# The first mixture of an attention and expert kernel in six units of unequal width instead of eight of 288 tokens

## The chip, the cores and the metric

The kernel runs on one core of one Trainium2 chip. The metric is the device time of one execution in microseconds; the time before is the median of three runs. The profile is of one execution of its own. PE is the matrix engine, PEld its weight load, DVE the vector engine, ACT the scalar engine, POOL the general engine and SP the engine that issues most DMAs.

## The reference

2304 tokens (4 batches of 576) go through three stages. Attention has 8 heads of 64; heads 0 to 3 see the last 32 positions, heads 4 to 7 every 32nd position. Then a dense mixture with 2048 hidden columns, then eight experts with 1024 hidden columns, one for each token.

```python
scores = np.where(masks[None, :, :, :], scale * np.matmul(q, k.transpose(0, 1, 3, 2)), -1000000000.0)
attn = np.exp(scores - np.max(scores, axis=-1, keepdims=True))
attn = attn / (np.sum(attn, axis=-1, keepdims=True) + 1e-09)
x = np.matmul(attn, v)                      # then heads side by side: 2304 x 512
r = np.maximum(x @ w_in, 0.0)               # first mixture, 512 x 2048
x = (s * (r * r) + b) @ w_out               # 2048 x 512
...
e_idx = np.argmax(x @ w_gate, axis=1)       # second: one of 8 experts a token
ye = np.maximum(x[mask] @ w1[e], 0.0) @ w2[e]
out[mask] = gate_w[mask, None] * eom[mask, e, None] * ye
```

## The kernel before

One Python generator stands for each stream of work, and a planner (`Order`, line 123) takes the operation that can begin first by its own table of costs and due times. It writes the instructions of every engine in that order, so each engine's order is fixed when the program is built, and the engines meet at semaphores.

**Attention** goes in 28 rounds, seven a batch (`rounds_of`, line 94): three strided ones ("S") of four blocks and four local ones ("L") of 3, 2, 2 and 2 blocks of 64 queries. A round (`attn`, line 426) has mask and score matmuls (L455 to L462), a softmax on DVE and ACT, transposes on PE (L511), the value product (L547, L549) and copies into `xsl`, high and low part (L572, L589). Rounds in `EXPB` take the exponentials on ACT, 64 or 96 columns at a time, the others in one piece with two more DVE operations. Rounds 7 and later are held back until a given step of the mixture has begun (`PACE1` to `PACE4`). The store `xsl` holds two batches of 576 columns, by the batch's parity.

**The first mixture** (`moe1`, line 696) works on units of U = 288 tokens, half a batch, eight of them, and for each unit on 16 blocks of 128 hidden columns, so 128 steps. A step is twelve matmuls into `h` (L713: four blocks of the depth by three passes, high by high, high by low, low by high) and, a step later, twelve into four accumulators (L743: again three passes). Between the two `chain` (L671) makes g = relu squared from h: ACT relu (L674), ACT square (L679), ACT copy that rounds to the high part (L686), DVE subtraction for the low part (L688). g comes from `NG` = 3 buffers, r from three. The weights come as 64-bit numbers and are cut to 32 bits and split by three to five DVE and ACT operations a tile (`split_w64`, L646 to L634); 32 tiles are needed in steps 0 to 23. Unit 0 does eight steps, then unit 1 all sixteen, then unit 0 the rest.

**After a unit** `finish` (L782) takes the four accumulators out (L803, L805), stores them, and `gates` (L815) splits each quarter to xh high and low (L824 or L826, L829), which takes a g buffer, multiplies it with the gate weights (L843, `wgt` of 128 columns of which 32 are used), and transposes the logits (L859). The planner puts a quarter's gate matmuls no sooner than `GLAT` after the split.

**The second mixture** (`dense`, line 1050) does one predicted expert for all tokens in groups of 384 (L1065 with 384 columns, L1090 and L1109 with 512 or 256); the rest of the tokens go through small extra work at the end.

**Idle PE** is filled by the planner with matmuls on zeros (`warm`, `filler`, L1399): 138 of 288 columns, all ahead of the first step.

Of the kernel before, what the change touches and what calls it, by code (L numbers as in the profile page):

```python
# [6 lines left out]
F32 = mybir.dt.float32  # L7
# [14 lines left out]
QT = 96  # L22
TPU = 3
# [7 lines left out]
PRED_UNIT = 4  # L31
# [11 lines left out]
U = S // 2  # L43
NU = NT // U
NEG = -8589934592.0
NQV = 2
NG = 3
# [22 lines left out]
EXPB = range(0, 14)  # L70
# [3 lines left out]
GLAT = 2.5  # L74
PACE1 = 9.0
PACE2 = 3.1
PACE3 = 28.0
PACE4 = 4.1
# [25 lines left out]
GPB = len(GROUPS) // B  # L104
# [134 lines left out]
def body(ctx, tc, qkv, w12, moe_s, moe_b, wg, e12, out):  # L239
# [8 lines left out]
    at = at_ctx.enter_context(tc.tile_pool(name="at", bufs=2))  # L248
    ps = enter(tc.tile_pool(name="ps", bufs=2, space=PSUM))

    xd = [dram.tile([P, KD, U], F32, name=f"xd{u}") for u in range(NU)]
# [13 lines left out]
    wgt = const.tile([P, KD, P], F32R, name="wgt")  # L265
# [9 lines left out]
    xsl = mx.tile([P, 8, 2, S], F32R, name="xsl", tag="big", bufs=1)  # L275
# [70 lines left out]
    t_g, t_r, t_raw, t_x1, t_x2 = Tok(NG), Tok(3), Tok(3), Tok(1), Tok(2)  # L346

    def prep():
        nc.vector.memset(ones, 1.0)
        nc.vector.memset(wgt.bitcast(F32), 0.0)  # L350
        one = mx.tile([P, P], F32, name="one", tag="r", bufs=3)
# [5 lines left out]
        mf = mx.tile([P, 2 * LK + QB], F32, name="mf", tag="r", bufs=3)  # L357
# [37 lines left out]
    for g, (kind, b, i0, n) in enumerate(GROUPS):  # L395
        us = {2 * b, 2 * b + 1}
        if kind == "L":
            us = {2 * b + i0 * QB // U, 2 * b + ((i0 + n) * QB - 1) // U}
        xuses.append(us)
        for u in us:  # L400
            left[u] += 1
# [18 lines left out]
    def xs(b):  # L420
        return xsl[:, 2 * (b % 2):2 * (b % 2) + 2, :, :]

    def xl(b):
        return xsl[:, 4 + 2 * (b % 2):6 + 2 * (b % 2), :, :]

    def attn(g):
# [13 lines left out]
        step = int(PACE1 + PACE2 * (g - GPB)) if g < 2 * GPB - 2 else int(PACE3 + PACE4 * (g - 2 * GPB + 2))  # L440
        step = -1 if g < GPB else step
# [22 lines left out]
        if g + 1 < len(GROUPS):  # L464
            o.spawn(attn(g + 1), prio=P_ATT if g + 1 < GPB else P_ATT2, pe=P_ATT)
# [32 lines left out]
        nt = n if strided else 2 * n  # L498
        yield op(("PE", nt * 0.09 + 0.02), waits=[singles if strided else pairs, t_w if early else t_ph])
        toks = o.got[0:1] if strided else o.got[0:2]  # L500
        ph, ph_tok = buf("ph")
        nj = n // 2 if strided else n
        ph = ph[:, 0:2 * nj * P].rearrange("p (h j k) -> p h j k", h=2, k=P)
        if strided:
            pt = banks_of(toks)[0].rearrange("p (h j k) -> p h j k", h=2, k=P)
        else:
            pt = two_banks(toks)[:, :, 0:nj * P].rearrange("p h (j k) -> p h j k", k=P)
        for j in range(nj):
            for h in range(2):
                src = pr[:, h, 2 * j:2 * j + 2, :].rearrange("p i k -> p (i k)") if strided else pr[:, h, j, :]  # L510
                nc.tensor.transpose(out=pt[0:nk, h, j, :], in_=src, identity=ident)  # L511
        o.free(pr_tok)
        yield op(("ACT", 2 * nj * P / 1200 + 0.19), ("DVE", 2 * nj * P / 960 + 0.12, P_EVAC), on=toks)
        if o.eng == "ACT":
            nc.scalar.activation(out=ph[0:nk], in_=pt[0:nk], func=AF.Copy)
        else:
            nc.vector.tensor_copy(out=ph[0:nk], in_=pt[0:nk])
        for tok in toks:
            o.free(tok)
        if strided:  # L520
            nq = [min(SQ, max(0, (STRIDE - (i0 + i) * CPB) * CLS)) for i in range(n)]
            last = 2 * b + 1
        else:
            nq = [QB] * n
            last = 2 * b + ((i0 + n) * QB - 1) // U
        deps = [ev_l1[last - 4]] if b >= 2 else []
# [32 lines left out]
        if strided:  # L559
            for r in range(2):  # L560
                r0 = (i0 + 2 * r) * CPB
                nr = sum(nq[2 * r:2 * r + 2]) // CLS
                src = ogs[r][:, 0:2 * P].rearrange("p (a x) -> p a x", a=2)[:, :, 0:nr * CLS]
                runs.append((toks[r], 2 * nr * CLS, src.rearrange("p a (r j) -> p a j r", j=CLS),
                             [xs(b)[:, hl].rearrange("q a (j r) -> q a j r", r=STRIDE)[:, :, :, r0:r0 + nr] for hl in range(2)]))
        else:
            src = ogs[0][:, 0:2 * n * QB].rearrange("p (a t) -> p a t", a=2)
            runs.append((toks[0], 2 * n * QB, src, [xl(b)[:, hl, :, i0 * QB:(i0 + n) * QB] for hl in range(2)]))
        for tok, nn, src, dst in runs:
# [20 lines left out]
            o.free(tok)  # L590
# [48 lines left out]
    def split_w64(j):  # L639
# [5 lines left out]
        a = mx.tile([P, 512], I32, name="w64", tag="wraw", bufs=3)  # L645
# [14 lines left out]
    def xt(u, c, hl):  # L660
        b, hf = divmod(u, 2)
        if c < 2:
            return xl(b)[:, hl, c, hf * U:(hf + 1) * U]
        return xs(b)[:, hl, c - 2, hf * U:(hf + 1) * U]

# [5 lines left out]
    def chain(k, u, h, ev, box):  # L671
        yield op(("ACT", 0.42), waits=[t_r])
        r = mx.tile([P, U], F32, name="r", tag="r", bufs=3)
        nc.scalar.activation(out=r, in_=h, func=AF.Relu)  # L674
        yield op(("DVE", 0.45), ("ACT", 0.43, P_SQ))
# [5 lines left out]
        yield op(("ACT", 0.43), waits=[t_g])  # L681
# [813 lines left out]
```

## Time and profile before

| what | us |
|---|---|
| median of three runs (733.22 to 733.96) | 733.46 |
| profiled execution, its own time | 732.7 |
| its span, first to last instruction | 731.0 |
| PE busy | 723.0 |
| DVE busy | 337.1 |
| ACT busy | 303.3 |
| first step of the first mixture starts at | 40.44 |
| second mixture starts at | 509.39 |

The span is read from the first instruction to the last. A group's row has its count, its busy time, the mean of one instruction and the idle time of the engine ahead of it with what ended it. A matmul's mean length is longer than the distance to the next one, since matmuls overlap; the distance is read from starts in the timeline. DMA packets took 26.4% of the 16 engines' span.

### The profile page before, as it was taken

Reading aid. Unit: us, or ns where it says so; the run is one execution under the profiler, and the core shown is the slowest. Engines: PE = TensorE matmul, PEld = TensorE weight load, DVE = VectorE, ACT = ScalarE, POOL = GpSimd, SP = SyncE. Lnnn points to the kernel's source line nnn. Section 1 sums busy time; section 2 is a strip of 40 time slices with the busy share of each in tenths; the row PEclk is TensorE's granted clock in tenths of the full one; section 3 lists DMA queues with packets and bytes.
Section 4 is the critical chain, followed back from the end, with each engine's and each line's share of the span. In section 5 each row is a group of like instructions: output and inputs, shape, how many; then the busy total and the mean of one; then the engine's idle time right before and its main releaser. Section 6 shows DMA issues by size and latency. Waiting matters only on the chain. (4 is left out here: it accounts for less than half of the span.)

```text
span 731.0 us, 14606 instructions
## 1 busy us (share of the span) xinstructions
PE 723.0 (99%) x5969; PEld 686.8 (94%) x5969; DVE 337.1 (46%) x818; ACT 303.3 (41%) x791; POOL 11.1 (2%) x67
## 2 busy tenths in 40 slices
PE   9999999999999999999999999999999999999996
PEld 7899999999999999999999999999999999888995
DVE  6998887444434434433542311751457513522220
ACT  5766655654445345444444444673221212111111
POOL 1000000000000000000000000000000000000001
PEclk9999999999999999999999999999999999999999
DMA  8953550303211122111100200560012297001011
GB/s 328 397 187 141 201 164 12 116 16 108 80 54 49 31 88 76 40 39 47 49 16 1 77 1 2 153 197 1 32 2 87 57 357 257 2 1 44 1 44 46
DMA packets 39113, 65.82 MB, mean 90 GB/s; under 512 B 12862, under 2 KB 21183, under 8 KB 39043
## 3 DMA queue, kind: packets, MB, share of 16 engines
q1 hardware_dynamic: 38882, 64.58, 26.4%
q8 instruction: 48, 0.79, 0.5%
q0 software_dynamic: 160, 0.28, 0.1%
q14 instruction: 23, 0.18, 0.1%
HBM read 54.64 MB, written 10.32 MB: 89 GB/s over the span
## 5 line engine op out<-in xcount | busy, mean ns | idle before, releaser
L713 PE MATMUL h<-xsl,w 128*128 128x288 f32 x1536 | 231.9, 297 | 0.0
L743 PE MATMUL bk<-g,w 128*128 128x288 f32 (+1 forms) x1524 | 230.4, 298 | 0.0
L713 PEld LDWEIGHTS h<-xsl,w 128*128 128x128 f32 x1536 | 211.5, 188 | 1.6
L743 PEld LDWEIGHTS bk<-g,w 128*128 128x128 f32 x1524 | 210.1, 189 | 2.1
L688 DVE TENSOR_TENSOR g<-r,g 128x288 fp32r<-128x288 f32 x128 | 58.6, 457 | 154.9 <-ACT g L686 141.7
L674 ACT ACTIVATE r<-h 128x288 f32<-128x288 f32 x128 | 52.6, 411 | 171.4 <-PE h L713 171.3
L1065 PE MATMUL h<-x,w 128*128 128x384 f32 x576 | 107.6, 336 | 0.0
L1065 PEld LDWEIGHTS h<-x,w 128*128 128x128 f32 x576 | 100.8, 188 | 3.2
L1090 PE MATMUL bk<-w,ht 128*128 128x512 f32 x360 | 90.8, 395 | 0.0
L1018 ACT ACTIVATE ht<-h 128x384 fp32r<-128x384 f32 x48 | 23.6, 491 | 149.7 <-PE h L1065 149.7
L1090 PEld LDWEIGHTS bk<-w,ht 128*128 128x128 f32 x360 | 66.5, 188 | 12.5 <-issue 0.6
L1020 DVE SCALAR_TENSOR_TENSOR ht<-h,ht 128x384 fp32r<-128x384 f32 x48 | 26.8, 558 | 102.1 <-ACT ht L1018 98.4
L686 ACT ACTIVATE g<-r 128x288 fp32r<-128x288 f32 x128 | 56.9, 444 | 14.7 <-PE bk L743 7.7
L679 ACT ACTIVATE r<-r 128x288 f32<-128x288 f32 x126 | 56.0, 444 | 3.9
L471 DVE TENSOR_REDUCE sm<-bk 128x4 f32<-128x384 f32 (+2 forms) x28 | 17.9, 641 | 27.3 <-PE bk L462 27.3
L479 ACT ACTIVATE pr<-bk,sm 128x64 f32<-128x64 f32 (+1 forms) x84 | 26.2, 329 | 0.3
L1399 PE MATMUL warm<-wgt 128*96 128x288 f32 x138 | 23.2, 316 | 1.7 <-DVE wgt L350 1.7
L1399 PEld LDWEIGHTS warm<-wgt 128*96 128x96 f32 x138 | 19.7, 173 | 2.7 <-DVE wgt L350 1.7
L649 DVE SCALAR_TENSOR_TENSOR w<-raw,w 128x512 int32<-128x512 int32 x32 | 21.9, 685 | 0.2
L652 DVE SCALAR_TENSOR_TENSOR w<-raw,w 128x512 int32<-128x512 int32 x32 | 21.9, 685 | 0.1
L549 PEld LDWEIGHTS bk<-ph,qkv 64*64 64x64 f32 (+1 forms) x600 | 17.4, 135 | 3.9 <-issue 2.1
L549 PE MATMUL bk<-ph,qkv 64*64 64x54 f32 (+1 forms) x600 | 20.8, 225 | 0.0
(175 smaller groups left out, 528.1 us busy)
## 6 DMA issues: line engine op xcount, KB each, us to landing
raw<-w SPq DMA_DIRECT2D x32, 512.0 KB, 8.0
qkv<-qkv SPq DMA_DIRECT2D x24, 256.0 KB, 2.9
qkv<-qkv SPq DMA_DIRECT2D x12, 512.0 KB, 4.8
xd<-x SPq DMA_DIRECT2D x8, 576.0 KB, 3.1
X<-xd SPq DMA_DIRECT2D x8, 576.0 KB, 7.3
out<-ob SPq DMA_DIRECT2D x17, 256.0 KB, 3.4
wraw<-e SPq DMA_DIRECT2D x16, 256.0 KB, 3.8
we<-e SPq DMA_DIRECT2D x8, 512.0 KB, 8.3
```

Of the source, the lines that this page charges most:

```text
L479: nc.scalar.activation(out=pr[:, h, i, :], in_=sc[:, h, i, :], func=AF.Exp, scale=0.125, bias=v[2][:, j:j + 1], accum_out=v[1][:, j:j + 1])
L549: nc.tensor.matmul(out=dst, lhsT=lhs, rhs=rhs)
L674: nc.scalar.activation(out=r, in_=h, func=AF.Relu)
L679: nc.scalar.activation(out=r, in_=r, func=AF.Square)
L686: nc.scalar.activation(out=gt[:, 0, 0:U], in_=r, func=AF.Copy)
L688: nc.vector.tensor_sub(out=gt[:, 1, 0:U], in0=r, in1=gt[:, 0, 0:U].bitcast(F32))
L713: nc.tensor.matmul(out=h, lhsT=w_t[2 * fc][:, a, c * P:(c + 1) * P], rhs=xt(u, c, x), start=(c == 0 and n == 0), stop=(c == KD - 1 and n = ...
L743: nc.tensor.matmul(out=acc[pu][c], lhsT=w_t[2 * pf + 1][:, a, c * P:(c + 1) * P], rhs=gt[:, x, 0:cols(pu)], start=(first and n == 0), stop ...
L1020: nc.vector.scalar_tensor_tensor(out=ht[:, 1, :], in0=h, scalar=0.0, in1=ht[:, 0, :].bitcast(F32), op0=ALU.max, op1=ALU.subtract)
L1065: nc.tensor.matmul(out=h, lhsT=w_t["p", 2 * fc][:, a, c * P:(c + 1) * P], rhs=x2[s][:, x, c, :], start=(c == 0 and n == 0), stop=(c == KD ...
L1090: nc.tensor.matmul(out=acc2[q][t][0], lhsT=pbox[0][:, x, t * P:(t + 1) * P], rhs=w_t["p", 2 * pf + 1][:, a, :], start=(pf == 0 and n == 0) ...
L1399: nc.tensor.matmul(out=t[0:3 * P // 4, 0:9 * P // 4], lhsT=wgt[:, 0, P // 4:], rhs=wgt[:, 0:3, P // 4:])
```

## The change

The eight units become six, of 288, 288, 384, 480, 384 and 480 tokens. Units 2 and later no longer end at batch borders, so a round's tokens can fall into two units. `xsl` is one strip of two regions: local heads 1056 columns, strided heads 1344, and `COL` says where each unit stands; units that are no longer read are overwritten, and `segments` gives for each round the pieces, their columns and the units that must be done before. Batches 1 to 3 have three local rounds of three blocks instead of four (25 rounds in all), and late local rounds transpose in two halves of one bank. A table `PACE` gives the step that holds each round back, and `EXPB` ends at round 9. The g, r and weight-raw buffers go from three to two. `GLAT` goes from 2.5 to 0.5. The unit's output tile `x1` gets a pool of its own, whose space the second x2 tile takes over after the last unit. The gate weights shrink to 32 columns, and the filler matmuls have 256 columns. Costs of operations in the planner follow the unit's width. The second mixture is as before.

```diff
-TPU = 3
+USZ = (288, 288, 384, 480, 384, 480)
+UOF = tuple(sum(USZ[:k]) for k in range(len(USZ) + 1))
+UMAX = max(USZ)
...
-NG = 3
+NG = 2
+NR = 2
+NRAW = 2
...
-EXPB = range(0, 14)
+EXPB = range(0,10)
...
-GLAT = 2.5
-PACE1 = 9.0
-PACE2 = 3.1
-PACE3 = 28.0
-PACE4 = 4.1
+GLAT = 0.5
+PACE = dict(zip(range(7, 25), (9, 12, 15, 18, 21, 32, 34, 36, 38, 40, 42, 48, 50, 53, 56, 59, 64, 69)))
...
+    even = [("L", b, i, 3) for i in (0, 3, 6)]
...
-    return early + strided + late if b == 0 else strided + early + late
+    return early + strided + late if b == 0 else strided + even
...
+WIDE = {"S": 1344, "L": 1056}
+COL = {"S": (192, 480, 864, 0, 480, 864), "L": (0, 288, 672, 96, 576, 0)}
...
+def segments(kind, t0, t1):
+
+    out = []
+    while t0 < t1:
+        u = unit_of(t0)
+        n = min(t1, UOF[u + 1]) - t0
+        c = COL[kind][u] + t0 - UOF[u]
+        dead = {v for v in range(u) if COL[kind][v] < c + n and c < COL[kind][v] + USZ[v]}
+        if out and out[-1][1] + out[-1][2] == c:
+            out[-1] = out[-1][0], out[-1][1], out[-1][2] + n, out[-1][3] | dead
+        else:
+            out.append((t0, c, n, dead))
+        t0 += n
+    return out
+
+
...
+    x1p = x1_ctx.enter_context(tc.tile_pool(name="x1p", bufs=1, side="right"))
...
-    wgt = const.tile([P, KD, P], F32R, name="wgt")
+    wgt = const.tile([P, KD, 4 * E], F32R, name="wgt")
...
-    xsl = mx.tile([P, 8, 2, S], F32R, name="xsl", tag="big", bufs=1)
+    xsl = mx.tile([P, 4 * sum(WIDE.values())], F32R, name="xsl", tag="big", bufs=1)
+    xk = {"S": xsl[:, 0:4 * WIDE["S"]].rearrange("p (c h t) -> p c h t", c=2, h=2),
+          "L": xsl[:, 4 * WIDE["S"]:].rearrange("p (c h t) -> p c h t", c=2, h=2)}
+
+    zero = xk["S"][:, 1, 1, COL["S"][2]:COL["S"][2] + 2 * P]
...
-        step = int(PACE1 + PACE2 * (g - GPB)) if g < 2 * GPB - 2 else int(PACE3 + PACE4 * (g - 2 * GPB + 2))
-        step = -1 if g < GPB else step
+        step = PACE[g] if g >= G1 else -1
...
+            halves = [(singles if strided else pairs, (0, 1))]
...
+            halves = [(singles, (0,)), (singles, (1,))]
+        for some, hs in halves:
...
-        deps = [ev_l1[last - 4]] if b >= 2 else []
+            segs = segments(kind, b * S + i0 * QB, b * S + (i0 + n) * QB)
+        deps = [ev_l1[u] for u in sorted(set().union(*(x[3] for x in segs)))]
...
+        kind = "L" if c < 2 else "S"
+        a = COL[kind][u]
+        return xk[kind][:, c % 2, hl, a:a + USZ[u]]
...
-        yield op(("ACT", 0.42), waits=[t_r])
-        r = mx.tile([P, U], F32, name="r", tag="r", bufs=3)
+        U = USZ[u]
+        yield op(("ACT", U / 1200 + 0.18), waits=[t_r])
+        r = mx.tile([P, UMAX], F32, name="r", tag="r", bufs=NR)[:, 0:U]
...
-        gt = mx.tile([P, 2, U + 2], F32R, name="g", tag="g", bufs=NG)
+        yield op(("ACT", U / 1200 + 0.19), waits=[t_g])
...
+            if u == NU - 1:
+                x1_ctx.close()
+                m2b.append(x2_ctx.enter_context(tc.tile_pool(name="m2b", bufs=1, side="right")))
+                o.set(ev_m2b)
...
-                x2[s] = m2[0].tile([P, 2, KD, SUP], F32R, name="x2", tag="x2", bufs=2)
+                x2[s] = (m2, m2b)[s % 2][0].tile([P, 2, KD, SUP], F32R, name="x2", tag="x2")
...
-            nc.tensor.matmul(out=t[0:3 * P // 4, 0:9 * P // 4], lhsT=wgt[:, 0, P // 4:], rhs=wgt[:, 0:3, P // 4:])
+            nc.tensor.matmul(out=t[:, 0:2 * P], lhsT=zero[:, 0:P], rhs=zero)
```

PE, near the end of the first mixture, one step. Before (`bk_842` to `bk_845` are the four accumulators):

```order
L713 MATMUL h<-xsl,w 128x288 x12
L743 MATMUL bk_842<-g,w 128x288 x3
L743 MATMUL bk_843<-g,w 128x288 x3
L743 MATMUL bk_844<-g,w 128x288 x3
L743 MATMUL bk_845<-g,w 128x288 x3
```

Now:

```order
L752 MATMUL h<-xsl,w 128x480 x12
L783 MATMUL bk_829<-g,w 128x480 x3
L783 MATMUL bk_830<-g,w 128x480 x3
L783 MATMUL bk_831<-g,w 128x480 x3
L783 MATMUL bk_832<-g,w 128x480 x3
```

The step is the same row by row, with 480 columns in place of 288; there are 96 steps instead of 128.

PE, the gates of a unit in the middle, between steps of the next (`xh` is the split output, `wgt` the gate weights, `pr` and `ph` belong to attention). Before, unit 4:

```order
L743 MATMUL bk_844<-g,w 128x288 x3
L743 MATMUL bk_845<-g,w 128x288 x3
L843 MATMUL bk_4859<-xh,wgt 128x288 x2
L713 MATMUL h<-xsl,w 128x288 x6
L843 MATMUL bk_4859<-xh,wgt 128x288 x2
L713 MATMUL h<-xsl,w 128x288 x6
L511 MATMUL bk_4976<-mk,pr 96x128 x4
L743 MATMUL bk_842<-g,w 128x288 x3
L743 MATMUL bk_843<-g,w 128x288 x3
L743 MATMUL bk_844<-g,w 128x288 x3
L743 MATMUL bk_845<-g,w 128x288 x3
```

Now, unit 3 of 480 tokens:

```order
L541 MATMUL bk_4252<-mk,pr 96x128 x3
L752 MATMUL h<-xsl,w 128x384 x6
L893 MATMUL bk_4251<-xh,wgt 32x480 x2
L581 MATMUL bk_4252<-ph,qkv 64x64 x12
L783 MATMUL bk_829<-g,w 128x384 x3
L783 MATMUL bk_830<-g,w 128x384 x3
L893 MATMUL bk_4251<-xh,wgt 32x480 x2
L783 MATMUL bk_831<-g,w 128x384 x3
L783 MATMUL bk_832<-g,w 128x384 x3
L752 MATMUL h<-xsl,w 128x384 x12
L893 MATMUL bk_4251<-xh,wgt 32x480 x2
L783 MATMUL bk_829<-g,w 128x384 x3
```

A quarter of the gates still takes two matmuls, and the quarters stand half a step to a whole step apart; the transposes of a round stand in two groups of three.

DVE, ahead of the first subtraction for g (first step of the mixture). Before (`raw` and `w` with numbers are weight tiles being cut and split):

```order
L1390 TENSOR_TENSOR wgt<-wgr,wgt 128x4x16
L634 TENSOR_TENSOR w<-w_708,w 128x512
L589 TENSOR_TENSOR xsl<-bk_761,xsl 128x2x128
L496 TENSOR_TENSOR pr<-pr,sm 128x384
L649 SCALAR_TENSOR_TENSOR w_773<-raw_483,w_773 128x512
L646 TENSOR_SCALAR w_819<-raw_612 128x512
L652 SCALAR_TENSOR_TENSOR w_773<-raw_483,w_773 128x512
L688 TENSOR_TENSOR g<-r,g 128x288
```

Now:

```order
L627 TENSOR_TENSOR xsl<-bk_108,xsl 128x2x128
L517 TENSOR_SCALAR sm<-sm 128x4
L518 RECIPROCAL sm<-sm 128x4
L673 TENSOR_TENSOR w<-w_639,w 128x512
L520 TENSOR_TENSOR pr<-pr,sm 128x384
L673 TENSOR_TENSOR w<-w_727,w 128x512
L685 TENSOR_SCALAR w_805<-raw_584 128x512
L1442 TENSOR_TENSOR wgt<-wgr,wgt 128x4x16
L727 TENSOR_TENSOR g<-r,g 128x288
```

Before, eleven weight tiles have been cut and a twelfth begun when the first g comes; now ten have been and an eleventh begun.

## Rows read from the trace of the kernel before

**Rows 1.** Page, parts 1 and 2: PE busy time, share, count; granted clock in tenths.

```profile
PE 723.0 (99%) x5969; PEld 686.8 (94%) x5969; DVE 337.1 (46%) x818; ACT 303.3 (41%) x791; POOL 11.1 (2%) x67
...
PEclk9999999999999999999999999999999999999999
```

**Rows 2.** Timeline of PE, first step of mixture one: start us, length us, instruction.

```profile
40.44 2.53 PE L713 MATMUL h<-xsl,w 128*128 128x288 f32 x18
```

**Rows 3.** Timeline of PE, twelve unbroken half steps, from first start to next start.

```profile
391.60 1.76 PE L713 MATMUL h<-xsl,w 128*128 128x288 f32 x12
...
410.73 1.74 PE L713 MATMUL h<-xsl,w 128*128 128x288 f32 x12
```

**Rows 4.** Timeline of PE, second mixture: 384 and 512 columns.

```profile
513.05 2.25 PE L1065 MATMUL h<-x,w 128*128 128x384 f32 x12
515.13 2.25 PE L1090 MATMUL bk<-w,ht 128*128 128x512 f32 x9
517.22 2.25 PE L1065 MATMUL h<-x,w 128*128 128x384 f32 x12
...
707.83 16.84 PE L1109 MATMUL bk<-w,ht 128*128 128x512 f32 x96
...
718.76 5.91 PE L1109 MATMUL bk<-w,ht 128*128 128x256 f32 x48
```

**Rows 5.** Timeline of PE, a local round of three blocks between half steps.

```profile
112.06 0.21 PE L455 MATMUL bk<-mk 128*128 128x96 f32 x1
...
112.57 0.73 PE L462 MATMUL bk<-qkv 64*64 64x96 f32 x24
...
114.94 1.76 PE L713 MATMUL h<-xsl,w 128*128 128x288 f32 x12
...
129.06 0.82 PE L511 MATMUL bk<-mk,pr 128*96 128x128 f32 x6
...
131.38 0.92 PE L549 MATMUL bk<-ph,qkv 96*64 96x64 f32 x24
...
133.93 1.75 PE L713 MATMUL h<-xsl,w 128*128 128x288 f32 x12
```

**Rows 6.** Timeline of PE, a local round of two blocks.

```profile
142.90 0.36 PE L457 MATMUL bk<-mk 128*128 128x192 f32 x2
143.19 0.56 PE L462 MATMUL bk<-qkv 64*64 64x96 f32 x16
...
145.37 1.74 PE L713 MATMUL h<-xsl,w 128*128 128x288 f32 x12
...
149.01 0.60 PE L511 MATMUL bk<-mk,pr 128*96 128x128 f32 x4
...
151.12 0.69 PE L549 MATMUL bk<-ph,qkv 96*64 96x64 f32 x16
...
153.43 0.36 PE L457 MATMUL bk<-mk 128*128 128x192 f32 x2
```

**Rows 7.** Groups by line and form, PE: count | busy us, mean ns | idle before, releaser.

```profile
L713 PE MATMUL h<-xsl,w 128*128 128x288 f32 x1536 | 231.9, 297 | 0.0
...
L743 PE MATMUL bk<-g,w 128*128 128x288 f32 x1332 | 200.9, 298 | 0.0
...
L843 PE MATMUL bk<-xh,wgt 128*128 128x288 f32 x64 | 12.3, 294 | 0.0
```

**Rows 8.** Groups by line and form, ACT and DVE, same columns.

```profile
L686 ACT ACTIVATE g<-r 128x288 fp32r<-128x288 f32 x128 | 56.9, 444 | 14.7 <-PE bk L743 7.7 <-DVE xh L829 1.0 <-ACT xh L824 0.6
...
L649 DVE SCALAR_TENSOR_TENSOR w<-raw,w 128x512 int32<-128x512 int32 x32 | 21.9, 685 | 0.2
...
L829 DVE TENSOR_TENSOR xh<-x,xh 128x288 fp32r<-128x288 f32 x32 | 13.9, 455 | 3.2 <-ACT xh L824 2.9
...
L824 ACT ACTIVATE xh<-x 128x288 fp32r<-128x288 f32 x19 | 7.9, 439 | 3.7 <-PE bk L843 2.0 <-PE bk L743 1.7
```

**Rows 9.** Busy us of each engine in a window: PE, PEld, DVE, ACT, POOL, clock, DMA.

```profile
30.00:40.00 10.00, 10.00 (x155) 8.89 (x153) 9.37 (x24) 7.81 (x38) 0.00 (x0) 1.00 0.92 343
```

More of the change, by code (lines that the diff above doesn't have):

```diff
@@ L345, in body @@
     t_sm = Tok(NSM)
-    t_g, t_r, t_raw, t_x1, t_x2 = Tok(NG), Tok(3), Tok(3), Tok(1), Tok(2)
+    t_g, t_r, t_raw, t_x1, t_x2 = Tok(NG), Tok(NR), Tok(NRAW), Tok(1), [Tok(1), Tok(1)]
     def prep():
         nc.vector.memset(ones, 1.0)
-        nc.vector.memset(wgt.bitcast(F32), 0.0)
-        one = mx.tile([P, P], F32, name="one", tag="r", bufs=3)
+        nc.vector.memset(zero.bitcast(F32), 0.0)
+        one = mx.tile([P, P], F32, name="one", tag="r", bufs=NR)
         nc.gpsimd.memset(one, 0.0)
@@ L508, in attn @@
[L508 to L517, printed above, removed]
@@ L518, in attn @@
-        for tok in toks:
-            o.free(tok)
+        if strided or early:
+            halves = [(singles if strided else pairs, (0, 1))]
+        else:
+            halves = [(singles, (0,)), (singles, (1,))]
+        for some, hs in halves:
+            nt = len(hs) * nj
+            yield op(("PE", nt * 0.09 + 0.02), waits=[some] + ([t_w if early else t_ph] if 0 in hs else []), dep=(0 in hs))
+            toks = [t for t in o.got if t in t_att or t in t_l2]
+            if 0 in hs:
+                ph, ph_tok = buf("ph")
+                ph = ph[:, 0:2 * nj * P].rearrange("p (h j k) -> p h j k", h=2, k=P)
+            if len(toks) == 2:
+                pt = two_banks(toks)[:, :, 0:nj * P].rearrange("p h (j k) -> p h j k", k=P)
+            else:
+                pt = banks_of(toks)[0][:, 0:len(hs) * nj * P].rearrange("p (h j k) -> p h j k", h=len(hs), k=P)
+            for j in range(nj):
+                for h in hs:
+                    src = pr[:, h, 2 * j:2 * j + 2, :].rearrange("p i k -> p (i k)") if strided else pr[:, h, j, :]
+                    nc.tensor.transpose(out=pt[0:nk, h - hs[0], j, :], in_=src, identity=ident)
+            if 1 in hs:
+                o.free(pr_tok)
+            yield op(("ACT", nt * P / 1200 + 0.19), ("DVE", nt * P / 960 + 0.12, P_EVAC), on=toks)
+            dst = ph[0:nk, hs[0]:hs[-1] + 1]
+            if o.eng == "ACT":
+                nc.scalar.activation(out=dst, in_=pt[0:nk], func=AF.Copy)
+            else:
+                nc.vector.tensor_copy(out=dst, in_=pt[0:nk])
+            for tok in toks:
+                o.free(tok)
@@ L589, in attn @@
                 nc.vector.tensor_sub(out=dst[1], in0=src, in1=dst[0].bitcast(F32))
-            o.free(tok)
+            if done:
+                o.free(tok)
         for u in xuses[g]:
@@ L798, in finish @@
                 continue
-            yield op(("ACT", 0.45), ("DVE", 0.45, P_EVAC), waits=[t_x1] if c == 0 else [], dep=(c == 0))
+            yield op(("ACT", U / 1200 + 0.2), ("DVE", U / 960 + 0.15, P_EVAC), waits=[t_x1] if c == 0 else [], dep=(c == 0))
             if c == 0:
-                x1 = mx.tile([P, KD, U], F32, name="x1", tag="x1", bufs=1)
+                x1 = x1_tile(u)
             if o.eng == "ACT":
@@ L820, in parts @@
             for c in range(KD):
-                yield op(("ACT", 0.33), ("DVE", 0.22), waits=[t_g], dep=False)
-                xh = mx.tile([P, 2, U], F32R, name="xh", tag="g", bufs=NG)
+                yield op(("ACT", U / 1200 + 0.1), ("DVE", U / 1920 + 0.08), waits=[t_g], dep=False)
+                xh = mx.tile([P, 2, UMAX], F32R, name="xh", tag="g", bufs=NG)[:, :, 0:U]
                 if o.eng == "ACT":
@@ L842, in gates @@
             for x in range(2):
-                nc.tensor.matmul(out=lt, lhsT=wgt[:, c, :], rhs=box[c][:, x, :],
+                nc.tensor.matmul(out=lt[0:4 * E], lhsT=wgt[:, c, :], rhs=box[c][:, x, :],
                                  start=(c == 0 and x == 0), stop=(c == KD - 1 and x == 1))
@@ L1409, in filler @@
                 for _ in range(n):
-                    nc.tensor.matmul(out=one_bank[id(tok)][0:3 * P // 4, 0:9 * P // 4], lhsT=wgt[:, 0, P // 4:], rhs=wgt[:, 0:3, P // 4:])
+                    nc.tensor.matmul(out=one_bank[id(tok)][:, 0:2 * P], lhsT=zero[:, 0:P], rhs=zero)
                 return
```

118 lines of the change are left out of this document (58 added, 60 removed).

## The prediction

> **What bounds the kernel now.** I read the page first: PE is busy 99% of the span, at the upper level of its clock in every slice [rows 1]; DVE and ACT are under half. The timeline of PE then has two parts. Up to 40.44 us [rows 2] PE does the first attention rounds, and zero matmuls fill the rest; DVE is the engine with the work there, 9.37 of 10 us busy just before the first step [rows 9]. From 40.44 us to the last matmul PE is not idle: the matmul groups of the first mixture have 0.0 us of idle time ahead of them [rows 7]. So from there the time is the sum of what PE issues, and a change counts by what it takes from that sum, as long as no new wait appears. The table of busy time can mislead here. A 288-column matmul has a mean length of 297 ns [rows 7], but the next one starts 133 ns later: twelve unbroken half steps of twelve matmuls go from 391.60 to 410.73 us, and 19.13 / 144 = 132.8 ns [rows 3]. I use such distances.
>
> **Fewer, wider matmuls.** At 2.4 GHz, 288 columns are 120.0 ns, so 12.8 ns of each distance do not go with the columns. If that part is fixed, it should be the same at other widths. 384 columns: (515.13 - 513.05) / 12 = 173.3 ns, 13.3 over 160.0. 512 columns in the last token group: (718.76 - 707.83) / 48 = 227.7 ns, 14.4 over 213.3. 512 columns in the other groups: (517.22 - 515.13) / 9 = 232.2 ns, 18.9 over [rows 4]. The first three agree on about 13 ns. The columns of the mixture stay: 2304 tokens, 16 blocks, 24 matmuls each. The matmuls go from 8 x 16 x 24 = 3072 to 6 x 16 x 24 = 2304, so 768 fewer. At 13 ns each that is **-10.0 us**. A 480-column matmul is not in the trace. It has the operands and the four accumulators of L713 and L743, so I take 13 ns; if it behaves like the 18.9 ns row, the 768 wide ones of the units of 480 pay 768 x 5.6 = 4.3 us more, which makes -5.7. All of this lies on the path.
>
> **Attention rounds.** A round interrupts the mixture three times. For a round of two blocks the stretches less the twelve 133 ns matmuls (1.59 us) in each are: scores 142.90 to 145.37, 2.47 - 1.59 = 0.88; transposes 149.01 to 151.12, 0.52; value product 151.12 to 153.43, 0.72; together 2.12 us [rows 6]. For three blocks: 112.06 to 114.94, 1.29; 129.06 to 131.38, 0.73; 131.38 to 133.93, 0.96; together 2.98 [rows 5]. That one starts a batch and has four mask matmuls in 0.51 us; a later round of three would have two as in rows 6, where they take 0.29, each 96 columns wider, so 0.37, and 2.84 in all. The local rounds of a batch go from 2.98 + 3 x 2.12 = 9.34 to 2.98 + 2 x 2.84 = 8.66, -0.68, and for three batches -2.0. Against it, the transposes stand in two groups in nine rounds. In rows 6 four transposes cost 0.52, about 0.44 for themselves at the pace of an added pair ((0.73 - 0.52) / 2 = 0.11 each), so a break costs about 0.08, nine of them 0.7. Sum **-1.3 us**, with -2.0 if a second group is free and about 0 if a break costs 0.2 us each time, as much as a whole pair of transposes. The strided rounds keep their matmuls; their copies in two pieces (one batch crosses a region's end) and the softmax of rounds 10 to 13 on DVE lie on engines that are under half busy.
>
> **Gates.** 64 matmuls become 48 [rows 7], 16 x 13 ns = **-0.2 us**. The columns are as many as before. What a weight tile of 32 columns changes is not in the trace; all 64 are 12.3 us of overlapping busy time, or 64 x 133 ns = 8.5 us of distance, so a tenth of it either way is 0.9 us, and I count nothing.
>
> **The start.** The first rounds are the same seven, and DVE has the work. Ahead of the first g, DVE does two fewer of the 0.685 us weight operations [rows 8], -1.4 us; the cast, the scalar operation and the memsets cancel within 0.1. The smaller fillers give nothing by themselves where PE waits for DVE. Whether the first step starts sooner depends on which of the last rounds' chains ends last. I take half, **-0.7 us**, between -1.4 and +0.8 (24 matmuls of h now stand ahead of a round's transposes, 18 before [rows 2], and six are 0.8 us). The weight work that is put off is done during the first steps, where the wait for it is hidden today; if it were not, the loss is the same 1.4 us again and the gain is zero.
>
> **Sum.** -10.0 - 1.3 - 0.2 - 0.7 = -12.2 us, made against the profiled execution of 732.7 us, hence 720.5 there; against the median of the runs, 733.46, **721.3 us**. Second mixture, extra work and the end are the same instructions in almost the same order, so they move as a block. The chains grow with the width, but so do the half steps that cover them: ACT copy and DVE subtraction are 0.444 and 0.455 us at 288 [rows 8] against a step of 24 x 133 ns = 3.2 us; at 480 the four chain operations are at most 480 / 288 times as long, and the step is 24 x 213 = 5.1 us, which is 1.6 times.
>
> **Rivals.** *Two buffers bring PE to a stop (slower).* g and the split quarters xh share the buffers, three before, two now. Already ACT waited 7.7 us in all for PE to give a g buffer back, and 2.0 us ahead of xh [rows 8]; these waits were hidden. With two, quarter c+1 can be split only when the gate matmuls of quarter c are done, so ACT copy 0.439 and DVE subtraction 0.455 [rows 8] stand in a row between two quarters. Against it: in the order the quarters stand at least twelve matmuls or half a step and a round's product apart, which is 1.6 us and more where the pair takes 0.9 (288) to 1.5 (480, by columns). It decides when the in-order queues of ACT or DVE have over a microsecond of something else (exponentials, weight splits) ahead of the pair. Fully exposed, 24 quarters cost 8 x (0.9 + 1.2 + 1.5) = 29 us, and the time is 750; from 12.2 / 24 = 0.5 us a quarter on it is slower than before. *Some quarters wait.* A third of them, by 0.6 us: +4.8, 726. The smaller `GLAT` speaks for it: the order leaves 2 us less between split and use. *The excess grows with the columns.* Rows 4 can also be read so: 12.8, 13.3, then 18.9. Then -5.7 for the first term, and 725.6. *The start gains all and a break is free.* 721.3 - 0.7 - 0.7 = 719.9. *The excess isn't fixed at all.* If most of the 13 ns is an effect of the stream (weight loads are busy beside it for 94% of the span [rows 1]) and a wider matmul brings it back in full, merging gives next to nothing: with a tenth to a fifth of it fixed, 1 to 2 us, the time is 729 to 730. The Trainium skill ("TensorE: Matmul & The Clock Gate", section "Wait — 56ns, not 53.3ns?") gives such a fixed part, about 2.5 ns over the columns' time for each warm matmul; by it the 768 matmuls are worth an estimated 1.9 us and the time would be 729.4. The 12.8 and 13.3 ns of rows 3 and 4 speak against it: the part over the columns' time is the same at 288 and at 384.
>
> **How the numbers follow.** Chances: the forecast 0.66, the better start 0.08, some quarters wait 0.12, the excess grows 0.06, not fixed 0.03, two buffers stop PE 0.05. The likeliest gives the predicted time. Its own bounds, and the next two cases, reach from 718.8 (all lower ends are -13.6 us, a little beyond for what the planner packs better) to 726.5, and leave out some 0.16. About 0.2%, 1.5 us, is what a measurement of this kernel can tell from no change. Slower comes from the two buffers alone, 0.05; within 0.2% from that case and from many waiting quarters together, 0.03; faster 0.92.
>
> **What would show it.** In the profile after: distance between starts of 480-column matmuls 213 ns (right) or 218 and more; 2304 matmuls in the two mixture lines with still 0.0 idle ahead of them; first step at 39 to 41 us; the gate line with no idle time of PE and no release by DVE xh (right) or with it (the buffers). Start of the second mixture should move from 509.39 by the same 12 us as the end; if it moves and the end doesn't, the late x2 tile or the extra work has become the bound, which I gave no chance of its own, since in the order six steps of token group 0, 6 x (2.08 + 2.09) = 25 us [rows 4], lie between the last gates and the first use of that tile. I am wrong if PE shows waits in the gate stretches, or if the start moves by over 1.5 us.

## The result, and the profile after

The changed kernel takes **724.2 us** (median of four runs, 723.94 to 724.54), the kernel before 733.48 beside it (733.22 to 733.96): ratio 0.9873, 95% interval 0.9856 to 0.989. It is faster by 9.3 us; the forecast was 721.3 us, 12.2 less than before, with a range of 718.8 to 726.5. The profiled execution took 724.54 us, 8.2 less than the one before.

The page and three groups of views answer to the rows ahead of the prediction. First the page: busy time of PE, and its clock in tenths in 40 slices.

```profile
PE 714.7 (99%) x5176; PEld 651.4 (90%) x5176; DVE 332.0 (46%) x770; ACT 277.9 (38%) x647; POOL 11.1 (2%) x67
...
PEclk9999999999999999999999999999999999999999
```

As in [rows 1], PE is the bound and its clock is at the upper level. The groups by line and form of the changed kernel (count | busy us, mean ns | idle before, releaser) answer to [rows 7, 8]:

```profile
L752 PE MATMUL h<-xsl,w 128*128 128x480 f32 x384 | 91.2, 382 | 0.0
...
L783 PE MATMUL bk<-g,w 128*128 128x480 f32 x372 | 87.3, 381 | 0.0
...
L893 PE MATMUL bk<-xh,wgt 128*32 128x480 f32 x16 | 4.5, 380 | 0.0
...
L725 ACT ACTIVATE g<-r 128x480 fp32r<-128x480 f32 x32 | 19.4, 605 | 6.4 <-PE bk L783 3.6 <-PE bk L893 1.9
...
L727 DVE TENSOR_TENSOR g<-r,g 128x480 fp32r<-128x480 f32 x32 | 21.0, 657 | 75.4 <-ACT g L725 75.4
```

The two product lines and the gates have 0.0 us idle ahead of them at every width (only the rows at 480 columns are shown): with two buffers PE still waits for nothing there. ACT waits for PE to give g back (3.6 and 1.9 us at 480), and PE doesn't wait for it. In the timeline of PE (start, busy us, operation, count) I read the first step, a round of three blocks, and unbroken stretches at each width; they answer to [rows 2 to 6]:

```profile
39.14 0.50 PE L1451 MATMUL warm<-xsl 128*128 128x256 f32 x2
39.48 3.33 PE L752 MATMUL h<-xsl,w 128*128 128x288 f32 x24
...
47.14 1.78 PE L783 MATMUL bk<-g,w 128*128 128x288 f32 x12
...
58.38 1.75 PE L752 MATMUL h<-xsl,w 128*128 128x288 f32 x12
...
141.08 0.96 PE L752 MATMUL h<-xsl,w 128*128 128x288 f32 x6
141.87 0.43 PE L481 MATMUL bk<-mk 128*128 128x288 f32 x2
142.23 0.73 PE L486 MATMUL bk<-qkv 64*64 64x96 f32 x24
142.89 1.88 PE L783 MATMUL bk<-g,w 128*128 128x288 f32 x12
144.60 0.96 PE L752 MATMUL h<-xsl,w 128*128 128x288 f32 x6
145.50 0.32 PE L909 MATMUL bk<-mk,lts 32*96 32x32 f32 x3
...
149.81 0.49 PE L541 MATMUL bk<-mk,pr 128*96 128x128 f32 x3
150.06 1.02 PE L783 MATMUL bk<-g,w 128*128 128x288 f32 x6
...
400.36 2.27 PE L783 MATMUL bk<-g,w 128*128 128x384 f32 x12
...
415.11 2.76 PE L752 MATMUL h<-xsl,w 128*128 128x480 f32 x12
...
439.95 2.76 PE L783 MATMUL bk<-g,w 128*128 128x480 f32 x12
...
479.09 2.78 PE L752 MATMUL h<-xsl,w 128*128 128x480 f32 x12
...
499.97 2.26 PE L1117 MATMUL h<-x,w 128*128 128x384 f32 x12
```

The first step starts at 39.48 us for 40.44, the second mixture at 499.97 for 509.39. Seven half steps at 288 columns take 58.38 - 47.14 = 11.24 us, 133.8 ns a matmul; seven at 384 take 415.11 - 400.36 = 14.75, **175.6 ns**; fifteen at 480 take 479.09 - 439.95 = 39.14, **217.4 ns**. The prediction wanted 173 and 213.

Where the time went, I summed over each trace: the distance from every matmul's start to the next one's, by line. From the first step to the last matmul there is hardly a wait, so this is the whole time there.

| us | before | after | measured | forecast |
|---|---|---|---|---|
| start to the first step | 40.44 | 39.48 | -0.96 | -0.7 |
| the two products of the first mixture | 417.69 | 412.68 | -5.01 | -10.0 |
| attention and the gates' transposes | 45.72 | 43.73 | -1.99 | -1.3 |
| gate matmuls | 8.43 | 8.77 | +0.34 | -0.2 |
| second mixture, extra work | 212.11 | 212.03 | -0.08 | 0 |
| from the last matmul to the end of the execution | 8.31 | 7.85 | -0.46 | 0 |
| the profiled execution | 732.70 | 724.54 | -8.16 | -12.2 |

The largest term was half of what was forecast, and smaller ones gave some of it back. The -0.08 of the second mixture is two changes that cancel: with the same instructions, its 384-column line went from 173.7 to 175.0 ns a matmul (+1.0 us in all) and its line with 360 matmuls of 512 columns from 231.3 to 229.1 (-1.0), so the distances there moved too, at other addresses. The medians differ by 1.1 us more than the profiled executions, since the one of before lies 0.8 below its median and the one of after 0.3 above.

### The profile page after: what moved, and what is told of

Same layout as the page of the kernel before. It is cut to its first block, busy times and chain, and to the rows that moved or that the text cites. A ratio compares the mean times of both kernels' runs of the same rounds, so it can differ in the third digit from the quotient of the medians.

```text
span 722.8 us, 12836 instructions
## 1 busy us (share of the span) xinstructions
PE 714.7 (99%) x5176; PEld 651.4 (90%) x5176; DVE 332.0 (46%) x770; ACT 277.9 (38%) x647; POOL 11.1 (2%) x67
## 5 line engine op out<-in xcount | busy, mean ns | idle before, releaser
L752 PE MATMUL h<-xsl,w 128*128 128x288 f32 (+2 forms) x1152 | 225.1, 341 | 0.0
L783 PE MATMUL bk<-g,w 128*128 128x384 f32 (+3 forms) x1140 | 219.9, 339 | 0.0
L752 PEld LDWEIGHTS h<-xsl,w 128*128 128x128 f32 x1152 | 190.3, 188 | 12.5
L783 PEld LDWEIGHTS bk<-g,w 128*128 128x128 f32 x1140 | 189.4, 188 | 12.6 <-ACT x L847 0.2
L713 ACT ACTIVATE r<-h 128x288 f32<-128x288 f32 (+2 forms) x96 | 47.2, 492 | 185.7 <-PE h L752 185.7
L727 DVE TENSOR_TENSOR g<-r,g 128x288 fp32r<-128x288 f32 (+2 forms) x96 | 53.4, 557 | 138.3 <-ACT g L725 137.7
L1142 PEld LDWEIGHTS bk<-w,ht 128*128 128x128 f32 x360 | 66.8, 188 | 11.7 <-issue 0.2
L725 ACT ACTIVATE g<-r 128x288 fp32r<-128x288 f32 (+2 forms) x96 | 50.4, 525 | 16.9 <-PE bk L783 9.1
L718 ACT ACTIVATE r<-r 128x288 f32<-128x288 f32 (+2 forms) x95 | 50.0, 526 | 3.0
L1451 PE MATMUL warm<-xsl 128*128 128x256 f32 x135 | 21.2, 305 | 1.4 <-DVE xsl L382 1.4
L1451 PEld LDWEIGHTS warm<-xsl 128*128 128x128 f32 x135 | 18.5, 205 | 2.7 <-DVE xsl L382 1.4
```

The source lines that it names most:

```text
L718: nc.scalar.activation(out=r, in_=r, func=AF.Square)
L725: nc.scalar.activation(out=gt[:, 0, 0:U], in_=r, func=AF.Copy)
L727: nc.vector.tensor_sub(out=gt[:, 1, 0:U], in0=r, in1=gt[:, 0, 0:U].bitcast(F32))
L752: nc.tensor.matmul(out=h, lhsT=w_t[2 * fc][:, a, c * P:(c + 1) * P], rhs=xt(u, c, x), start=(c == 0 and n == 0), stop=(c == KD - 1 and n = ...
L783: nc.tensor.matmul(out=acc[pu][c], lhsT=w_t[2 * pf + 1][:, a, c * P:(c + 1) * P], rhs=gt[:, x, 0:cols(pu)], start=(first and n == 0), stop ...
L1142: nc.tensor.matmul(out=acc2[q][t][0], lhsT=pbox[0][:, x, t * P:(t + 1) * P], rhs=w_t["p", 2 * pf + 1][:, a, :], start=(pf == 0 and n == 0) ...
```

## Experiments

The theory that I took from the traces: the part of a distance above columns / 2.4 GHz is not fixed but grows with the width, so the merging is worth 5 us, and the rest of the 8 to 9 us is rounds, start and end. The rival is the prediction's own: 13 ns fixed, 10 us from the merging, and 3 us lost to something else, a neighbour in the memories or a wait.

**Widths by themselves.** Nothing runs but PE, in the operand patterns of the two products.

```diff
...
+for n in (288, 320, 352, 384, 416, 448, 480, 512):
+    h_run(n)     # one accumulator, four x blocks, three passes: 96 matmuls
+    y_run(n)     # four accumulators, one g
+for n in (288, 384, 480, 512):
+    h_run(n, x0=141632 + 32)
+    y_run(n, g0=188224 + 32)
...
```

> The kernel leaves out everything that the reference computes (the output is zeros): PE does runs of 96 fp32r matmuls, first with the operand pattern of the mixture's first product (one accumulator, four x blocks), then of the second (four accumulators, g), at 256, 288, 320, 352, 384, 416, 448, 480 and 512 columns, at the addresses that the changed kernel uses; 288, 384, 480 and 512 come again with the moving operand 32 bytes further on, and 384 and 480 with a plane stride of 2048 bytes. Read is the distance between starts. Theory 'fixed' (the prediction's): columns / 2.4 plus 13 to 14 ns at every width, so 133, 173, 213, 227 ns at 288, 384, 480, 512; what the changed kernel shows at 480 (217 to 219) would then come from something else that runs beside it. Theory 'width': the part above the columns' time grows, 12.7, 15.5, 17.2 ns at 288, 384, 480 and more at 512, wherever the operands lie. Theory 'layout': the part differs by 3 ns or more between runs of one width that differ only in address or pattern, and is 13 ns in the best of them.

The timeline of PE of this kernel, a row a run (from 60 us on DVE, ACT and POOL have no instruction, and DMA brings only instructions, 16 KB at a time; the granted clock is 1.00):

```profile
60.68 12.80 PE L288 MATMUL h<-sb 128*128 128x288 f32 x96
73.32 12.86 PE L294 MATMUL y<-sb 128*128 128x288 f32 x96
...
114.18 15.52 PE L288 MATMUL h<-sb 128*128 128x352 f32 x96
129.54 15.52 PE L294 MATMUL y<-sb 128*128 128x352 f32 x96
144.90 16.81 PE L288 MATMUL h<-sb 128*128 128x384 f32 x96
161.54 17.01 PE L294 MATMUL y<-sb 128*128 128x384 f32 x96
178.39 18.24 PE L288 MATMUL h<-sb 128*128 128x416 f32 x96
...
253.96 20.96 PE L288 MATMUL h<-sb 128*128 128x480 f32 x96
274.76 20.96 PE L294 MATMUL y<-sb 128*128 128x480 f32 x96
295.56 21.97 PE L288 MATMUL h<-sb 128*128 128x512 f32 x96
317.37 22.14 PE L294 MATMUL y<-sb 128*128 128x512 f32 x96
339.34 12.96 PE L288 MATMUL h<-sb 128*128 128x288 f32 x96
...
440.58 22.56 PE L288 MATMUL h<-sb 128*128 128x512 f32 x96
462.98 22.57 PE L294 MATMUL y<-sb 128*128 128x512 f32 x96
```

A row's start to the next row's, over 96: 131.7 ns at 288 (11.7 over the columns' time), 160.0 at 352 (13.3 over), 173.3 and 175.5 at 384 (13.3 and 15.5), 216.7 and 216.7 at 480 (**16.7**), 227.2 and 228.9 at 512 (13.9 and 15.5). With the moving operand 32 bytes further on, 512 columns take (462.98 - 440.58) / 96 = 233.3 ns, 20.0 over. Other runs gave 11.1 to 13.3 at 256, 15.0 to 15.5 at 416, 16.7 to 20.0 at 448, and up to 20.0 at 480. So 'width' and 'layout' each hold in part: at 480 none came below 16.6, while at 384 and 512 the address decides between about 13 and 17 or 20, and 512 columns at their best address are less over than any run at 480. 'Fixed' falls. The distances are not noise; they repeat in patterns of 3, 6 or 12 matmuls (221, 213, 220, 213, 221, 212 at 480).

**The changed kernel's own addresses, still with nothing beside PE**, then other plane distances (from the high to the low part of g) and another order of the passes.

```diff
...
+for u in range(6):
+    h_run(u)          # x of unit u, where the changed kernel has it
+    y_run(USZ[u])
+for plane in (1952, 1984, 2016, 2048, 2080, 2112, 2144):
+    y_run(384, plane)
+    y_run(480, plane)
...
```

> The kernel leaves out everything that the reference computes (the output is zeros): PE does runs of 96 fp32r matmuls with the very operand addresses of the changed kernel, unit by unit (x in its two regions, then g), then with the distance between the hi and the lo plane of g at 1952 to 2144 bytes instead of 1920, with the regions of x widened by 8 to 24 columns, and with the three passes in another order. First it should give the part above the columns' time of the changed kernel again, 12.9, 15.6 and 17.2 ns at 288, 384 and 480, with nothing running beside; then no other engine has a part in it. Theory 'layout': the part at 480 comes down to 13 to 14 ns at some plane distance or order, by 3 ns, and the changed kernel could have had the whole of the forecast gain by other addresses. Theory 'width': at 480 nothing comes below 16 ns, as in the first probe (16.6 to 20.0), while 384 moves between 13.3 and 16.6.

```profile
59.73 6.75 PE L290 MATMUL h<-sb 128*128 128x288 f32 x49
66.31 12.89 PE L297 MATMUL y<-sb 128*128 128x288 f32 x96
79.05 12.88 PE L290 MATMUL h<-sb 128*128 128x288 f32 x96
91.77 12.86 PE L297 MATMUL y<-sb 128*128 128x288 f32 x96
104.46 17.06 PE L290 MATMUL h<-sb 128*128 128x384 f32 x96
121.36 17.01 PE L297 MATMUL y<-sb 128*128 128x384 f32 x96
138.21 21.01 PE L290 MATMUL h<-sb 128*128 128x480 f32 x96
159.06 20.96 PE L297 MATMUL y<-sb 128*128 128x480 f32 x96
179.86 17.03 PE L290 MATMUL h<-sb 128*128 128x384 f32 x96
```

In the timeline of PE, again a row a run (the first is the rest of one, 49 matmuls): 134.3 and 132.7 ns for the first unit of 288, 132.5 and 132.2 for the second, 176.0 and 175.5 at 384, 217.2 and 216.7 at 480. At 384 and 480 this is the changed kernel's own to 0.5 ns (means of its distances away from interruptions, first and second product: 175.6 and 175.6, 217.7 and 216.7), without DVE, ACT or any DMA but instruction loads. At 288 the kernel has 132.6 and 132.2 in the first product, 134.0 and 133.5 in the second, so the probe is off by up to 2 ns there. The lost 5 us, which lie at the two wide widths, need no neighbour. At 480 the other planes and orders gave 15.5 to 18.4 ns over, at 384 14.1 to 16.4.

**The merging undone.** Eight units of 288 again, the six rounds of each later batch and the two buffers kept.

```diff
-USZ = (288, 288, 384, 480, 384, 480)
+USZ = (288,) * 8
...
```

> The changed kernel with the merging alone undone: eight units of 288 tokens again, so 3072 matmuls in the mixture's two lines and 64 in the gates, with six rounds, two buffers and the rest kept (columns of the regions and the steps of the rounds moved to fit). Theory 'fixed' (the prediction's term of -10.0 and -0.2 us for the merging): 724.2 + 10.2 = 734.4 us. Theory 'the distance's excess grows with the width' (distances read in the two traces: 408.2 us of undisturbed matmuls before, 403.7 after, gates 8.4 against 8.8): 724.2 + 4.2 = 728.4 us.

It took **733.82 us** (732.94 to 735.22). By the time alone 'fixed' would have won, 734.4 to 728.4. The trace says otherwise. The two products take 417.77 us, 5.1 more than the 412.68 of the changed kernel and not 10, and 0.8 of the 5.1 is waiting (the first row below); the 4.3 without it are near the 4.2 of the second theory. The other 4.7 us of the profiled executions (734.1 against 724.3 of the same program as the changed kernel run beside it) are: first step 39.83 for 39.20 us, 0.6; attention 1.8, most of it at two waits (the records show 0.9 idle there, but a matmul's record is longer than the distance to the next one); from the last matmul to the end 10.05 for 7.89 us, 2.2. The waits are in the groups by line and form:

```profile
L783 PE MATMUL bk<-g,w 128*128 128x288 f32 x1332 | 200.7, 297 | 0.8 <-ACT x L847 0.6 <-DVE x L837 0.2
...
L541 PE MATMUL bk<-mk,pr 128*96 128x128 f32 x72 | 11.6, 275 | 0.6 <-ACT ph L547 0.6
```

The end is in the view of DMA for the 6 us around the last plain store (40 slices of GB/s; then bytes and busy share of 16 engines by queue; then us to landing):

```profile
GB/s 0 0 0 0 0 0 0 0 0 0 0 0 0 109 150 382 369 369 300 69 0 0 0 0 14 14 14 0 27 27 14 0 0 0 0 0 0 0 0 0
...
q8 instruction: 1, 0.02, 1.6%
...
out<-ob SPq DMA_DIRECT2D x1, 256.0 KB, 3.8
```

One instruction load (1.6% of 16 x 6 us is 1.5 us of one engine) begins just ahead of the store. Nearly all of the store is written by slice 20; a few packets follow in slices 25 to 31. In the packet records the load goes from 720.07 to 721.62 us and the first late packet begins at 721.61, so I take them to have stood behind it; no run tests this. The store lands after 3.8 us. The same view of the changed kernel:

```profile
GB/s 0 0 0 0 0 0 0 0 0 0 0 0 0 0 0 0 0 0 96 396 382 355 396 123 0 0 0 0 0 0 0 0 0 0 109 0 0 0 0 0
...
q8 instruction: 1, 0.02, 1.0%
...
out<-ob SPq DMA_DIRECT2D x1, 256.0 KB, 2.0
```

Here the load comes after the store, which lands in 2.0 us. What follows waits for the landing: POOL writes the extra work's rows, and 2.93 us after that (in every trace) the last tile's rows. In the changed kernel this last write begins at 717.88 us, 0.4 after ACT has the tile ready; in the run of eight units 2.3 us after.

**Three buffers with units of 288**, to tell whether the waits are those of two buffers. The buffers hold 290 columns here and 480 in the run above, so addresses differ too.

```diff
...
-NG = 2
-NR = 2
-NRAW = 2
+NG = 3
+NR = 3
+NRAW = 3
...
```

> The run with eight units of 288 once more, now with three buffers for each step (g and xh, r, the split weights) as in the kernel before; with units of 288 they fit. In the run with two buffers PE waited 1.7 us in the records (0.8 ahead of the second product, 0.9 in the attention), and the first step began at 39.83 us. If two buffers cause these waits, they go, and the last matmul starts 1.5 us earlier, at about 722.5 us; if the order made by other units causes them, they stay and it starts at 724 us as before. On the rounds: without the waits this kernel differs from the one before by the six rounds, the 32-column gate weights and the start alone, so by the traces so far it should have its last matmul 2 us ahead of the 724.39 of the kernel before (rounds -2.4, gates about +0.1, start -0.6 and the waits); if the rounds are worth the 1.3 us of the prediction, 1 us ahead. The time itself also holds the end: it is longer by about 1.5 us if an instruction load meets the last plain store.

732.39 us (731.84 to 733.52), ratio to the kernel before 0.9989 (0.998 to 0.9998). The waits went but for 0.2 us ahead of the second product: attention with the gates' transposes takes 43.72 us for 45.50. But the last matmul starts at 723.63 and not at 722.5: the first step comes 0.4 us later (40.27), the planner put six matmuls on zeros into a gap (0.8 us), and the second mixture is 0.4 us longer (0.55 against the kernel before), by the distances at its new addresses. The two products take 417.76 us, as with two buffers. So with units of 288 the missing third buffer, or the order that the planner makes without it, cost 1.8 us in the attention; with the wide units PE waited for nothing. The six rounds, against the kernel before, took 2.0 us from the attention.

**The rounds undone**: 3, 2, 2 and 2 blocks in the later batches again.

```diff
...
-    return early + strided + late if b == 0 else strided + even
+    return early + strided + late if b == 0 else strided + early + late
...
```

> The changed kernel with the rounds alone undone: the later batches have local rounds of 3, 2, 2 and 2 blocks again, 28 rounds in all for 25, transposes of a round of two in one group. By the prediction's term the rounds are worth 1.3 us (bounds 0 to 2.0), so 725.5 us. By the two traces (attention operations 45.6 against 43.6 us on PE, and 0.6 us less in the matmuls behind them) they are worth 2.6 us, so 726.8 us. If a gap in time between the two kernels that is put down to the rounds belongs to the width instead, this run is at 724.2.

729.49 us (729.02 to 729.91), 5.0 more than the 724.47 of the same program as the changed kernel beside it; more than either theory. Its trace has the attention 1.7 us longer, the two products 0.8 by more interruptions, the gates 0.3 shorter, nine zero matmuls of the planner, 1.2; and the end 9.72 for 7.89 us, by a store that lands after 3.5 us (the largest of the last stores and writes):

```profile
DMA to landing us min/median/max: 2.0/2.4/3.5
```

So the rounds are worth 2.1 us on PE in this order (attention, products and gates together), and the rest is that same end and the zero matmuls.

**The transposes in one group again**, six rounds a batch kept.

```diff
-        if strided or early:
-            halves = [(singles if strided else pairs, (0, 1))]
-        else:
-            halves = [(singles, (0,)), (singles, (1,))]
+        halves = [(singles if strided else pairs, (0, 1))]
```

> The changed kernel with the transposes of a round in one group again (a pair of banks, as before), six rounds kept; PE order changes with it in the planner's hands. The prediction charged each of the nine added breaks 0.08 us, 0.7 in all: by that the last matmul starts 0.7 us earlier. By a count in the trace of the changed kernel, group by group and with the longer first matmul behind it, two groups of three transposes cost 0.33 us each and one of six 0.66, so a break is free: no change, unless waiting for two free banks costs something.

724.25 us; from the first step to the last matmul 676.76 us for 677.21. PE waits for nothing in either trace, so 0.45 us is what the nine breaks and the changed order cost together. In the timeline of PE a group of six, 151.94 to 152.51, is 0.57 us, and the changed kernel's group of three, 149.81 to 150.06 above, 0.25; with the 0.08 us by which the next product matmul is late, 0.66 and twice 0.33: by this count a break is free.

```profile
151.94 0.82 PE L538 MATMUL bk<-mk,pr 128*96 128x128 f32 x6
152.51 1.03 PE L749 MATMUL h<-xsl,w 128*128 128x288 f32 x6
```

**Another plane distance for g in the changed kernel**, the best one of the probe.

```diff
...
-        gt = mx.tile([P, 2, UMAX], F32R, name="g", tag="g", bufs=NG)
+        gt = mx.tile([P, GPL + UMAX], F32R, name="g", tag="g", bufs=NG)
+        gt = gt[:, 0:GPL], gt[:, GPL:GPL + UMAX]
...
```

> The changed kernel with one edit: the two planes of g lie 2080 bytes apart instead of 1920 (the second product's moving operand); nothing else differs, PE has the same matmuls in the same order. In the probe of plane distances this was the best for both widths: 215.5 ns at 480 columns for 216.7, 175.2 at 384 for 175.5. If a distance is set by width and address alone, the second product's line shows these two values with all other engines at work, the first product's line stays at 217.6 and 175.5, and the last matmul starts 384 x 1.2 + 384 x 0.3 ns = 0.6 us earlier. If neighbours on other engines set it, nothing moves. The time: 723.8 us, inside what the measurement can tell from 724.4.

A miss. 725.04 us, and PE's sum from the first step to the last matmul is 677.89 us for 677.21. The second product went from 175.6 to 175.1 ns at 384, as the probe said, but from 216.7 to **217.6** at 480 where 215.5 was expected, and the second mixture's 512-column matmuls went from 229.1 to 231.4. Their code didn't change, but g's buffers grew from 3840 to 4000 bytes, so what lies behind them moved: the edit did more than the expectation says. Address moves the distance by 1 to 3 ns, and the probe didn't tell how for the kernel. The probe has eight weight tiles where the kernel has 32, and no run varied the weights' addresses. What in the address does it stays open.

**Both kernels once more.**

> The changed kernel once more, beside the others on one chip: 724.2 us, and the same distances in the trace to within 0.1 ns in the mean of a line. A difference of more than 0.7 us to 724.2 would mean that differences of that size between chips or runs carry no meaning here.

724.47 us (724.3 to 724.9), the first step at 39.20, from there to the last matmul 677.21 us as in the first trace of the changed kernel, and the same mean in both product lines at each width to 0.05 ns.

> The kernel before once more, for a second trace of it. Its profiled execution took 732.7 us while the median of its runs is 733.4, and single runs lie between 732.6 and 734.2. If the end makes that spread, PE's sum from the first step to the last matmul is 683.95 us again to within 0.1, and a longer time shows as a later landing of the last plain store (2.05 us after its issue in the first trace) or as a later first step (40.44). If PE itself is longer, the sum shows it.

732.26 us; 683.92 us from the first step to the last matmul for 683.95, first step at 40.39, the last store lands after 2.04 us. PE's part repeats to 0.05 us. Of the 0.44 us between the two traces 0.38 lie behind the start of the last write, from which it is 5.30 and 4.92 us to the end of the span. Both traces of the kernel before have the early landing and lie at the low side of its runs (732.26 to 734.23). That the others have the late one would explain the 0.8 us, but no trace of such a run was taken, so this stays open.

No run was measurably faster than the changed kernel.

## Why the prediction was right, and which of its terms were not

**The mechanism** held: PE's sum bounds the kernel, the groups show 0.0 idle, and the second mixture moved with the end, by 9.4 us at its start and 7.7 at the last matmul; the difference is the last half step and the gates of the wider last unit, which fall behind the first step of the second mixture.

**Fewer, wider matmuls** is the term that was mis-sized: -10.0 forecast, -5.0 measured, beyond even the bound of -5.7. The step that failed is to take 13 ns for every width. It leaned on 13.3 ns at 384 in twelve matmuls of the second mixture [rows 4], which the probe shows to be the low end of 13.3 to 16.6 for that width, and took the 18.9 of a 512 row as the exception, where that width gives 13.9 to 20.0 by its address. With the measured 12.8, 15.6 and 17.2 ns the term is 768 x (12.8 + 15.6 + 17.2) = 35.0 us against 3072 x 12.8 = 39.3 us, -4.3. Another 0.6 us is gone because fewer of the distances that interruptions lengthen lie in these two lines (9.4 us before, 8.8 now). The bound charged the 480-wide ones alone; the 384-wide ones pay too. This was the rival "the excess grows with the columns", priced at 725.6 us and given 0.06: the case given 0.66 did not come.

**The opposite rival**, next to nothing fixed, 729 to 730 us, is out: a line drawn from 132.9 ns at 288 to 217.2 at 480 meets zero columns at 6.4 ns, which is an estimate of the fixed part. The Trainium skill ("TensorE: Matmul & The Clock Gate", section "Wait — 56ns, not 53.3ns?") would have 2.5 ns there; the measurement decides for the larger part in this stream.

**Attention rounds**: -1.99 us for -1.3. The 0.7 for two local rounds of three in place of three of two was right for each batch (counted by groups with the matmul behind: 3 x 2.05 = 6.15 against 2 x 2.73 = 5.46, 0.69). The 0.7 us for nine breaks was too much: 0.45 by the run without them, the changed order included, and nothing by the count of a group with the matmul behind it. The 0.08 read from [rows 6] for a break is the longer distance ahead of the value product at the end of that stretch, which a second group does not repeat.

**Gates**: +0.34 for -0.2. There are 16 fewer, but as the part over the columns' time grows here too (131.8 ns at 288 before; 133, 175 and 218 at the three widths now) this is worth nothing, and four of the 48 now stand beside an interruption, one behind and three ahead of it, where a distance is 0.08 to 0.10 us longer: 0.36 us. Of the 32-column weight tile nothing over 1 ns is seen: 288 columns take 133 ns.

**The start**: -0.96 (-1.24 in the second trace) for -0.7. DVE's busy time ahead of the first step went from 33.19 to 31.97 us, three operations fewer, and PE followed nearly in full. Two traces of the same program differ by 0.28 us here, so it is not shown closely how much of it PE gets; the half that I took was on the careful side.

**Two buffers bring PE to a stop**, the rival on the slow side, did not happen, nor did some quarters wait. The reason given, that the half steps grow with the chain, fits: the ACT copy of g took 0.605 and the DVE subtraction 0.657 us at 480. The run with narrow units and two buffers did wait, 1.7 us in its records from the first step on, and with three buffers 0.2.

**The end** was said to move as a block. Up to the last write it does within 0.1 us: the write starts 1.28 us after the last matmul before, 1.19 now. The other 0.37 of the 0.46 us lie behind its start (5.30 us to the end of the span, now 4.94), and the second trace of the kernel before has 4.92 there, so they belong to that one execution and not to the change. A chain that I hadn't priced can move the end by 2 us, as two runs above show: last store, extra write, last write.

Sum of the terms: -8.2 us between the two profiled executions for -12.2. The time fell in the range because the range had taken in the growth of the excess, but it was in part luck that it came so near: the rounds and the start gave 1 us more than forecast, and the medians lie 1.1 us further apart than the traces, which no run explains.

## What to carry to other kernels

Read the distance between matmuls at the very width and address at which it will be used, or measure it alone; here one number taken over from another line was off by 2 to 4 ns, and 768 fewer matmuls were worth 5 us and not 10. Below one per cent, compare sums over a trace and not times: the run with the merging undone was 9.4 us slower, nearly as the wrong theory said, with some 4 us of it from waits and from a late store. Ask of each kernel what its last write waits for.

## What the hardware showed that was not expected

- The distance of fp32r matmuls is columns / 2.4 GHz and 11 to 20 ns, by width and by address, in fixed patterns, with no other engine at work: 11.1 to 13.3 at 256, 11.7 to 14.3 at 288, 13.3 at 320 and 352, 13.3 to 16.6 at 384, 15.5 to 20.0 at 480, 13.9 to 20.0 at 512. Many runs lie at just 13.3, 16.7 or 20.0, which is the time of 32, 40 or 48 columns at 2.4 GHz; why stays open.
- An interruption of the first mixture lengthens a distance by 80 to 110 ns at one or two places: at the first product or gate matmul behind it (71 times in each kernel), and at the last one ahead of it where a value product or the logits' transposes come (27 times before, 24 now), but not ahead of masks or a round's transposes. In the rows above, six matmuls ahead of masks take 141.87 - 141.08 = 0.79 us and six ahead of the logits' transposes 145.50 - 144.60 = 0.90. In all it is 9.4 us before and 9.1 now.
- An instruction load of 16 KB holds one DMA engine for 0.9 to 1.6 us. In the two traces where one begins just ahead of the last store's packets (eight units; rounds undone), the store lands after 3.8 and 3.5 us instead of 2.0, and from the last matmul to the end it is 2.2 and 1.8 us longer. That the load is the cause is read from the times of the packets, not tested.
